# Attention with gradients on one core: o is added up two units later, one VectorE copy takes out o and dQ, and GpSimd scales dQ

## The chip, the core and the metric

The kernel runs on one core of a Trainium2 chip. A core has five engines that work side by side, each through its own queue of instructions, in the order in which they were written: TensorE (PE in the profile, its weight loads PEld), VectorE (DVE), ScalarE (ACT), GpSimd (POOL) and SyncE (SP, which here only issues DMAs). An engine waits on a semaphore when an instruction needs what another engine has not finished yet, and everything behind that instruction in the same queue waits with it. The metric is the device time of one execution in microseconds (us); less is better.

## The reference

The program computes an output and all gradients of two attention blocks that share a gradient `grad_out`: block A is linear attention, block B is softmax attention with 16 heads of 28 columns that share one K and one V (multi-query). The change touches block B alone:

```python
q = (x @ wq).reshape(B, S, H, Dh)      # S = 2048, H = 16, Dh = 28
k = x @ wk
v = x @ wv
scores = einsum("bhqd,bkd->bhqk", q, k) * Dh ** -0.5
p = softmax(scores)
o = einsum("bhqk,bkd->bhqd", p, v)
out = o.reshape(B, S, H * Dh) @ wo
```

and its backward pass: dP = dO v^T, dS = p * (dP - D) with D the row sum of dO * o, then dQ = scale * dS k, dK = dS^T q, dV = p^T dO, and the gradients of x and of the weights from them.

## The kernel before, in words

Up to about 230 us the kernel does block A and the projections of block B. Then comes the loop that the change is in (lines 905 to 1008), and after it the last weight gradients and dx (lines 1010 to 1090).

The loop works on 64 **blocks**. A block is one chunk of 256 query rows (`qc`) for one pair of heads (`pair`), numbered b = 8 qc + pair. A block takes eight **units**, one for each 256 keys (two tiles of 128). The loop variable is the unit u, and the whole order of the work is written out by hand: the loop stands in a manual schedule, each engine gets its instructions in the order of the lines, and each step has a **lag**. `due(u, lag)` gives block b when u = 8b + lag. Steps of different blocks so meet in one unit. Because the schedule repeats every eight units, it is enough to follow units 8 to 15 of a block; unit 16 is unit 8 of the next one. A step at lag 20 of one block falls in the same unit as lag 12 of the next.

What one unit u does:

- **TensorE**, first `rows_SD` (663): four matmuls for the scores S of unit u into two of three PSUM banks `SB`, and four for dP of unit w = u - 16 into the two banks `DB`. The third SB bank of the unit is called `spare`. Then on even units the first `o_dq` (914), then `onat_T` and `don_T` if they are due, then an output projection if one is due. After that, on odd units, four `dk_m` (984) for dK; on even units the second `o_dq` (986) and the `dv_mm` for dV (989).
- **ScalarE**: exp of the first score bank (927), a copy `cp` of the second half of dP (941), exp of the second score bank (973). These are the tiles `eT`, `cp`, `eT`.
- **VectorE**: dS = dP * eT for the first half of dP (939, out of the bank DB[0]), then the small steps that are due, and last a transpose of the dS tile of unit u - 18 into `dsx` (1006).
- **GpSimd**: dS for the second half, `cp` * eT (942), then the small steps that are due; in some units a copy of q (833).
- **SyncE**: every fourth unit a DMA transpose of four `eT` tiles into `eN` (975), which dV reads, and now and then others (837, 964).

The steps that take results out, for block b, with their lags before the change:

- `o_mm` (850) adds p v for unit u - 2 (first `o_dq` of an even unit) or u - 1 (second), into rows 0 to 63 of the one PSUM tile `oq`; row 0 of each head is the softmax's sum. `dq_mm` (859) adds dS k for units u - 20 and u - 19 into rows 64 to 127 of `oq`. The two take turns, so that four matmuls of 32 columns each lie beside each other.
- lag 9: VectorE copies o, 64 rows by 256, from `oq` to the SBUF tile `oTs` (955).
- lag 10: `onat_T` (788) transposes it on TensorE into the spare bank; `o_norm` (795) takes the reciprocal of the sums (800), multiplies by it and writes the normalized o into `oTs[:, 0:128]` (801, VectorE), and then on GpSimd makes `prod` = dO * o (805), `don` = dO / sum (808), and copies o over dO in `do_nat` (809).
- lag 12: `row_D` (811) sums `prod` on VectorE (813) and writes D / sum into a column of `don` on GpSimd (814). I call this last small product **Dmul**.
- lag 14: `don_T` (816) transposes `don` on TensorE into the spare bank (822), and VectorE copies the result to `doT` (829). The dP matmuls of the block begin at unit 16 and read `doT`.
- lag 20, 20, 22 and 26: the four `dv_mm` of a block (987 to 989), which read `don` and `eN`.
- lag 27: VectorE scales dQ, 64 rows by 256, out of rows 64 to 127 of `oq` into `qT_B` (958).

`oTs` has one buffer, `DB` has two banks, `SB` three.

Of the kernel before, what the change touches and what calls it, by code (L numbers as in the profile page):

```python
# [9 lines left out]
ALU = mybir.AluOpType  # L10
# [6 lines left out]
D = 448  # L17
P = 128
# [7 lines left out]
def kernel(  # L26
# [21 lines left out]
    nc = tc.nc  # L48
# [3 lines left out]
    scale = float(DH) ** -0.5  # L52
# [574 lines left out]
    NB = 64  # L627
    NU = NB * 8
    qT_B = [R1[:, g, :] for g in range(4)]
    vaug, kn, do_nat = vaug_, kn_, R2x[:, 0:NS, :]  # L630
    with ExitStack() as cs_:
# [11 lines left out]
        oq, dk_acc = (psA.tile([P, 512], F32, name="agen") for _ in range(2))  # L643

        dsT, dsx, qX, don, doT, rl, prod = ({} for _ in range(7))
# [3 lines left out]
        def eT(u):  # L649
            return ETs[u // 4 % 5][:, u % 4, :, :]  # L650

        def eN(b, c):
            return ENs[(2 * b + c // 2) % 6][:, 16 * (c % 2):16 * (c % 2) + 16, :]

        def mmt(out, lhsT, rhs, pos, start, stop):
            nc.tensor.matmul(out, lhsT=lhsT, rhs=rhs, start=start, stop=stop, tile_position=pos,  # L656
                             skip_group_check=True)

        def blk(b):
            qc, pair = divmod(b, 8)  # L660
            return qc, pair, pair // 2, pair % 2
# [29 lines left out]
        identF = pp_.tile([P, P], F32, name="identF", bufs=1)  # L691
        make_identity(nc, identF[:])
        oTs = pp_.tile([P, 256], F32, name="oTs", bufs=1)
# [3 lines left out]
        outs = {}  # L697
# [4 lines left out]
        for n in range(7):  # L702
            q_ = n + (n > 5)
            outs[400 + 8 * n] = (8 + q_ // 4, q_ % 4 * W4 - (n == 6) * W4, (q_ % 4 + 1) * W4)
        outs.update({456 + 8 * n: (10 + n // 2, n % 2 * (D // 2), (n % 2 + 1) * (D // 2)) for n in range(8)})

        def out_part(u):
            if u in (532, 536):
# [70 lines left out]
                        nc.gpsimd.dma_start(out_8[h * DH:(h + 1) * DH, :], sb[32 * j + 1:32 * j + 1 + DH, :])  # L779

        GW = [0, 0, 4, 4, 10, 10, 16, 16, 22, 22, 28, 28, 34, 34, 40, 40, 48, 48, 56, 56, 64, 64]
        onps, tps2 = {}, {}

        def due(u, lag):
            b, r = divmod(u - lag, 8)
            return b if r == 0 and 0 <= b < NB else None

        def onat_T(b, bank):
            onp = bank[:, 0:P].rearrange("p (q h c) -> p q h c", q=2, h=2)
            for qb in range(2):  # L790
                nc.tensor.transpose(onp[:, qb, :, :].rearrange("p h c -> p (h c)"), oTs[0:64, qb * P:(qb + 1) * P],
                                    identF[0:64, 0:64], tile_position=(0, 0))
            onps[b] = onp

        def o_norm(b):
            onp = onps.pop(b)
            qc, pair, g, hp = blk(b)
            r_ = pw_.tile([P, 2, 2, 1], F32, name="rl")
            os_ = oTs[:, 0:P].rearrange("p (q h c) -> p q h c", q=2, h=2)
            nc.vector.reciprocal(out=r_[:], in_=onp[:, :, :, 0:1])  # L800
            nc.vector.tensor_tensor(out=os_, in0=onp[:, :, :, :], in1=r_[:].to_broadcast([P, 2, 2, 32]), op=ALU.mult)  # L801
            rl[b] = r_
            dnv = do_nat[:, 2 * qc:2 * qc + 2, pair * 64:pair * 64 + 64].rearrange("p q (h c) -> p q h c", c=32)
            prod[b] = pw_.tile([P, 2, 2, 32], F32, name="prod", bufs=1)
            nc.gpsimd.tensor_tensor(out=prod[b][:], in0=dnv, in1=os_, op=ALU.mult)  # L805
            dn = pw_.tile([P, 2, 2, 32], BF16, name="don", bufs=3)
            don[b] = dn
            nc.gpsimd.tensor_tensor(out=dn[:], in0=dnv, in1=r_[:].to_broadcast([P, 2, 2, 32]), op=ALU.mult)
            nc.gpsimd.tensor_copy(out=dnv, in_=os_)

        def row_D(b):
            Dq = pw_.tile([P, 2, 2, 1], F32, name="Dq")
            nc.vector.tensor_reduce(out=Dq[:, :, :, 0], in_=prod[b][:], axis=AX.X, op=ALU.add)
            nc.gpsimd.tensor_tensor(out=don[b][:, :, :, 0:1], in0=Dq[:], in1=rl[b][:], op=ALU.mult)
# [16 lines left out]
        def qc_copy(eng, st, qc, g, s):  # L831
            src = qT_B[g][:, qc * 256:(qc + 1) * 256].rearrange("p (b j s) -> p b j s", b=4, s=2)[:, :, :, s]
            eng.tensor_copy(out=st.rearrange("p (b s) a j -> p b s a j", s=2)[:, :, s, :, :],  # L833
                            in_=src.unsqueeze(2).to_broadcast([P, 4, 4, 32]))
# [15 lines left out]
        def o_mm(v):  # L850
            b, tp = divmod(v, 8)
            for t2 in range(2):
                t = 2 * tp + t2
                for h in range(2):
                    mmt(oq[32 * h:32 * h + 32, 0:256], vaug[:, t, :],
                        eT(v)[:, h, t2 * 256:(t2 + 1) * 256], (0, 32 * h), t == 0, t == 15)
                yield

        def dq_mm(y):
            b, tp = divmod(y, 8)  # L860
            for t2 in range(2):
                t = 2 * tp + t2
                for h in range(2):
                    mmt(oq[64 + 32 * h:96 + 32 * h, 0:256], kn[:, t, :],
                        dsT[y][:, h, t2 * 256:(t2 + 1) * 256], (0, 64 + 32 * h), t == 0, t == 15)
                yield

        def o_dq(vs, ys):
            for v, y in zip(vs, ys):
                todo = [f(i) for f, i in ((o_mm, v), (dq_mm, y)) if 0 <= i < NU]  # L870
                for _ in range(2):
                    for g_ in todo:
                        next(g_)

        def dv_mm(dv_acc, b, h, qb):
            for c in range(4):
                rhs = eN(b, c).rearrange("p (u h t q) k -> p u h t q k", u=2, h=2,
                                                       t=2)[:, :, h, :, qb, :]
                mmt(dv_acc[32 * c:32 * c + 32, :], don[b][:, qb, h, :], rhs, (0, 32 * c),
                    b == 0 and h + qb == 0, b == NB - 1 and h + qb == 2)  # L880
# [15 lines left out]
        with tc.manual_schedule():  # L896
# [8 lines left out]
            for u in range(NU + 28):  # L905
# [5 lines left out]
                dp = DB if hasD else None  # L911
                rows_SD(u, sp, dp)
                if u % 2 == 0:
                    o_dq((u - 2,), (u - 20,))
                if (b := due(u, 10)) is not None:
                    onat_T(b, spare)
                if (b := due(u, 14)) is not None:
                    don_T(b, spare)
# [9 lines left out]
                if u == 1:  # L928
                    q_shift(pn3, shifts[3], [pd_.tile([P, 2, 512], BF16, name="dsT").rearrange("p a b -> p (a b)").bitcast(F32)
                                             for _ in range(1)])  # L930
                    dv_acc = psA.tile([P, 512], F32, name="aacc")
# [13 lines left out]
                if 0 <= gq < 4 and u < 448:  # L945
                    if gq == 0 and iq == 0:
                        qX[qq] = (pqb_ if qq % 2 else pqa_).tile([P, 4, 2, 512], BF16, name="qX")
                    if iq < 2:
                        qc_copy(nc.gpsimd, qst, qq, gq, iq)
                if (b := due(u, 12)) is not None:  # L950
                    row_D(b)
                if u == 7:
                    nc.vector.memset(oTs[64:128, :], 0.0)
                if (b := due(u, 9)) is not None:
                    nc.vector.tensor_copy(out=oTs[0:64, :], in_=oq[0:64, 0:256])  # L955
                if (b := due(u, 27)) is not None:
                    qc, pair, g, hp = blk(b)
                    nc.vector.tensor_scalar(out=qT_B[g][64 * hp:64 * hp + 64, qc * 256:(qc + 1) * 256],  # L958
                                            in0=oq[64:128, 0:256], scalar1=scale, scalar2=None, op0=ALU.mult)
                if (b := due(u, 10)) is not None:  # L960
                    o_norm(b)
                    if b in (15, 31, 47, 55, 63):
                        t0, t1 = 2 * (b // 8) - 2 * (b < 48), 2 * (b // 8) + 2
                        nc.sync.dma_start_transpose(oTq[:, 4 * (t0 % 4):4 * (t0 % 4) + 4 * (t1 - t0), :],
                                                    do_nat[:, t0:t1, :].rearrange("p q c -> p (q c)"))
# [14 lines left out]
                if u % 2:  # L980
                    b, i = divmod(u - 27, 8)
                    if 0 <= b < NB:
                        for m in range(2 * i, 2 * i + 4):
                            dk_m(b, m)
                else:
                    o_dq((u - 1,), (u - 19,))
                    b, n = divmod(u - 20, 8)
                    for k in {0: (0, 1), 2: (2,), 6: (3,)}.get(n, ()) if 0 <= b < NB else ():
                        dv_mm(dv_acc, b, k // 2, k % 2)
                y = u - 18  # L990

                if 512 <= u < 530 and u % 2 == 0:
# [9 lines left out]
                if 0 <= y < NU:  # L1002
                    b, tp = divmod(y, 8)
                    if tp == 0:
                        dsx[b] = px_.tile([P, 8, 2, 2, 256], BF16, name="dsx")
                    nc.vector.transpose(  # L1006
                        out=dsx[b][:, tp, :, :, :].rearrange("p h t c -> p (h t c)").bitcast(F32),
                        in_=dsT[y][:, :, :].rearrange("p h c -> p (h c)").bitcast(F32))
# [16 lines left out]
        for c in range(4):  # L1025
            t = dkvT[0:32, :].rearrange("p (t a i) -> p t a i", a=4, i=32)[:, :, c, :]
# [52 lines left out]
        for c in range(4):  # L1079
            r = DC_ROWS[c]  # L1080
# [41 lines left out]
```

## Time and profile before

| what | value |
|---|---|
| median of 3 runs | 1066.74 us (1066.0 to 1067.32) |
| the profiled execution: its time | 1067.99 us |
| its span, first to last instruction | 1066.3 us |
| mean granted TensorE clock | 0.998 |
| TensorE busy | 1042.2 us (98%) |
| VectorE busy | 896.1 us (84%) |
| ScalarE busy | 873.7 us (82%) |
| GpSimd busy | 781.3 us (73%) |
| first and last copy of o (line 955) start at | 230.3 and 994.5 us |

The profile's page lists busy time by engine, the span in 40 slices, the DMA queues, the chain that ended last and the costliest groups of instructions by line. A trace behind it gives each instruction's start and duration in order of time (the timeline) and what an engine waited for. Two cautions for reading it. Busy time counts the whole of each instruction, from start to finish, and consecutive instructions of one engine overlap: in the loop ScalarE starts a new instruction every 0.48 us though each is listed with some 0.6 us. So distances between starts say more than busy shares. And the 64 starts of a line that runs once in a block give the length of a block: (994.5 - 230.3) / 63 = 12.13 us.

### The profile page before, as it was taken

The page shows a single profiled execution, that of the slowest core. Times are in us where ns is not written, and L with a number is a line of the kernel's source. Part 1 is how long each engine was busy: PE and PEld are TensorE (multiplying, and loading weights), DVE is VectorE, ACT ScalarE, POOL GpSimd, SP SyncE. Part 2 cuts the span into 40 slices and gives each one's busy share as a digit, 9 for nine tenths or more (in the row PEclk, how much of TensorE's full clock was granted, in tenths as well). Part 3 has the DMA queues.
Part 4 walks back from the last instruction along what each step waited for, and adds up shares of the span by engine and source line. Part 5 has one row for each costly group of instructions (what it writes and reads, how often), then busy time and mean ns, then how long its engine had stood idle before and what let it go on. Part 6 is the DMA issues. An engine that isn't in the chain of part 4 may idle for free.

```text
span 1066.3 us, 39861 instructions
## 1 busy us (share of the span) xinstructions
PE 1042.2 (98%) x16241; PEld 476.1 (45%) x16241; DVE 896.1 (84%) x1797; ACT 873.7 (82%) x1741; POOL 781.3 (73%) x1033
## 2 busy tenths in 40 slices
PE   9999999999999999999999999999999999999998
PEld 5555555433444444444444444444444444444434
DVE  7888400459999999999999999999999999999943
ACT  6454122479999999999999999999999999999622
POOL 6001242227988898899889989988998999888881
PEclk9999999999999999999999999999999999999999
DMA  9749899079999999999999999999999999999963
GB/s 267 163 95 200 161 214 250 21 138 168 192 202 198 170 203 187 195 191 193 196 186 189 197 192 198 185 191 194 195 195 195 195 191 186 206 191 179 218 141 92
DMA packets 689936, 195.14 MB, mean 183 GB/s; under 512 B 670616, under 2 KB 687792, under 8 KB 689752
## 3 DMA queue, kind: packets, MB, share of 16 engines
q1 hardware_dynamic: 680152, 179.92, 99.2%
q0 software_dynamic: 4640, 8.71, 2.8%
q10 hardware_dynamic: 4960, 3.96, 1.3%
q8 instruction: 127, 2.08, 0.7%
q14 instruction: 57, 0.47, 0.1%
HBM read 12.60 MB, written 10.84 MB: 22 GB/s over the span
## 4 chain that ended last, share of the span: by engine, by line
PE 52%; DVE 35%; POOL 4%; issue 4%; ACT 3%; DMA 1%; DVEq 0%; POOLq 0%; ACTq 0%
PE agen L656 20%; PE agen L81 15%; DVE dsT L939 14%; DVE dsx L1006 12%; PE aacc L656 9%; PE aacc L81 7%; POOL dsT L942 4%; DVE R L958 2%; DVE oTs L801 2%; DVE oTs L955 2%; ACT cp L941 1%; DVE rl L800 1%; ACT eT L973 1%; DMA dsx<-R 1%; ACT eT L927 0%
## 5 line engine op out<-in xcount | busy, mean ns | idle before, releaser
L942 POOL TENSOR_TENSOR dsT<-cp,eT 128x512 bf16<-128x512 bf16 x512 | 588.1, 1157 | 77.3 <-ACT cp L941 68.9
L1006 DVE STREAM_TRANSPOSE dsx<-dsT 128x512 f32<-128x512 f32 x512 | 356.4, 696 | 2.4 <-POOL dsT L942 0.2
L656 PEld LDWEIGHTS <-R 32*128 32x128 bf16 (+1 forms) x9104 | 215.5, 93 | 318.3 <-issue 293.0
L939 DVE TENSOR_TENSOR dsT<-agen,eT 128x512 bf16<-128x512 f32 x512 | 338.5, 661 | 11.7 <-PE agen L656 8.4
L941 ACT ACTIVATE cp<-agen 128x512 bf16<-128x512 f32 x512 | 324.7, 634 | 12.5 <-PE agen L656 12.5
L927 ACT ACTIVATE eT<-aacc 128x512 bf16<-128x512 f32 x512 | 324.0, 633 | 11.6 <-PE aacc L656 4.7
L973 ACT ACTIVATE eT<-aacc 128x512 bf16<-128x512 f32 x512 | 330.6, 646 | 0.0
L656 PE MATMUL agen<-doT,R 32*128 32x256 bf16 x2048 | 270.9, 269 | 10.9 <-DVE dsT L939 8.2
L656 PE MATMUL aacc<-R,R 32*128 32x256 bf16 (+1 forms) x2240 | 269.7, 268 | 2.7 <-ACT eT L927 0.8
L656 PE MATMUL agen<-dsx,qX 32*32 32x512 bf16 x4096 | 267.7, 375 | 0.0
L656 PE MATMUL agen<-eT,R 128*32 128x256 bf16 x2048 | 182.0, 276 | 0.1
L656 PE MATMUL agen<-dsT,R 128*32 128x256 bf16 x2048 | 181.4, 276 | 0.1
L656 PEld LDWEIGHTS <-qX 32*32 32x32 bf16 x4096 | 79.7, 89 | 114.9 <-issue 54.3
L656 PE MATMUL aacc<-eN,don 128*32 128x512 bf16 x1024 | 97.6, 379 | 0.0
L81 PEld LDWEIGHTS <-R 128*128 128x128 bf16 (+1 forms) x517 | 41.0, 99 | 42.9 <-issue 11.1
L406 POOL COPY pk<-R 128x256 bf16<-128x256 bf16 x4 | 1.6, 397 | 75.3 <-DVE R L366 75.3
L81 PE MATMUL agen<-R,R 128*128 128x448 bf16 (+1 forms) x180 | 42.4, 363 | 0.3 <-ACT R L225 0.3
L833 POOL COPY qst<-R 128x512 bf16<-128x512 bf16 x56 | 34.2, 611 | 4.8 <-DMA qX<-qst 4.6
L805 POOL TENSOR_TENSOR prod<-R,oTs 128x128 f32<-128x128 bf16 x64 | 27.5, 430 | 9.8 <-DVE oTs L801 9.8
L656 PEld LDWEIGHTS <-don 128*32 128x32 bf16 x1024 | 34.2, 97 | 0.8
L422 DVE TENSOR_TENSOR osb<-aacc,pr 64x448 bf16<-64x448 f32 x2 | 1.2, 617 | 37.9 <-DMA out_dram<-osb 24.0
L958 DVE TENSOR_SCALAR R<-agen 64x256 bf16<-64x256 f32 x64 | 27.3, 426 | 3.6 <-PE agen L656 1.6
(231 smaller groups left out, 971.1 us busy)
## 6 DMA issues: line engine op xcount, KB each, us to landing
out_dram<-osb ACTq DMA_DIRECT2D x22, 112.0 KB
eN<-eT SPq DMA_TRANSPOSE x128
xa<-in_A_x_dram SPq DMA_DIRECT2D x8, 224.0 KB
ga<-in_grad_out_dram SPq DMA_DIRECT2D x4, 448.0 KB
xa<-in_grad_out_dram POOLq DMA_DIRECT2D x4, 448.0 KB, 5.7
out_dram<-wdq POOLq DMA_DIRECT2D x8, 224.0 KB, 3.8
eT<-in_grad_out_dram SPq DMA_DIRECT2D x4, 448.0 KB
eT<-in_B_x_dram SPq DMA_DIRECT2D x4, 448.0 KB
```

What stands on the lines that cost most here:

```text
L81: nc.tensor.matmul(out_ap, lhsT=lhsT, rhs=rhs, start=start, stop=stop, tile_position=(0, 0))
L656: nc.tensor.matmul(out, lhsT=lhsT, rhs=rhs, start=start, stop=stop, tile_position=pos, skip_group_check=True)
L801: nc.vector.tensor_tensor(out=os_, in0=onp[:, :, :, :], in1=r_[:].to_broadcast([P, 2, 2, 32]), op=ALU.mult)
L805: nc.gpsimd.tensor_tensor(out=prod[b][:], in0=dnv, in1=os_, op=ALU.mult)
L833: eng.tensor_copy(out=st.rearrange("p (b s) a j -> p b s a j", s=2)[:, :, s, :, :], in_=src.unsqueeze(2).to_broadcast([P, 4, 4, 32]))
L927: nc.scalar.activation(out=eT(u)[:, 0, :], in_=sp[0][:, :], func=ACT.Exp, scale=scale)
L939: nc.vector.tensor_tensor(out=dst[:, 0, :], in0=dp[0][:, :], in1=ew[:, 0, :], op=ALU.mult)
L941: nc.scalar.activation(out=cp[:, :], in_=dp[1][:, :], func=ACT.Copy)
L942: nc.gpsimd.tensor_tensor(out=dst[:, 1, :], in0=cp[:, :], in1=ew[:, 1, :], op=ALU.mult)
L958: nc.vector.tensor_scalar(out=qT_B[g][64 * hp:64 * hp + 64, qc * 256:(qc + 1) * 256], in0=oq[64:128, 0:256], scalar1=scale, scalar2=None, ...
L973: nc.scalar.activation(out=eT(u)[:, 1, :], in_=sp[1][:, :], func=ACT.Exp, scale=scale)
L1006: nc.vector.transpose(out=dsx[b][:, tp, :, :, :].rearrange("p h t c -> p (h t c)").bitcast(F32), in_=dsT[y][:, :, :].rearrange("p h c -> p ...
```

## The change

The diff does five things.

1. `o_mm` is done two units later: `o_dq` is called with u - 4 and u - 3 in place of u - 2 and u - 1. With that o of block b and dQ of block b - 2 are finished in the same unit. The half of `oq` that each uses alternates: o of an even block goes to rows 64 to 127 and of an odd one to rows 0 to 63, dQ to the other half.
2. At lag 11 one VectorE copy of 128 rows by 256 takes both from `oq` to `oTs`. It stands in place of the copy at lag 9 and of the scaling at lag 27. GpSimd then scales dQ of block b - 2 from `oTs` (SBUF, float32) into `qT_B`; for the last two blocks VectorE still does it out of PSUM.
3. `onat_T` and `o_norm` move from lag 10 to 12, `row_D` from 12 to 13. `don_T` and the copy to `doT` stay at lag 14.
4. The copy of o over dO in `do_nat` leaves `o_norm` and is a step of its own at lag 14 (`o_keep`); the DMA transposes of `do_nat` (five in all) move with it. Eight of the output projections start 8 units later.
5. The first `dv_mm` of a block moves from lag 20 to 18.

```diff
-        outs.update({456 + 8 * n: (10 + n // 2, n % 2 * (D // 2), (n % 2 + 1) * (D // 2)) for n in range(8)})
+        outs.update({464 + 8 * n: (10 + n // 2, n % 2 * (D // 2), (n % 2 + 1) * (D // 2)) for n in range(8)})
...
         def onat_T(b, bank):
             onp = bank[:, 0:P].rearrange("p (q h c) -> p q h c", q=2, h=2)
+            r = 64 * (1 - b % 2)
             for qb in range(2):
-                nc.tensor.transpose(onp[:, qb, :, :].rearrange("p h c -> p (h c)"), oTs[0:64, qb * P:(qb + 1) * P],
-                                    identF[0:64, 0:64], tile_position=(0, 0))
+                nc.tensor.transpose(onp[:, qb, :, :].rearrange("p h c -> p (h c)"), oTs[r:r + 64, qb * P:(qb + 1) * P],
+                                    identF[r:r + 64, r:r + 64], tile_position=(r, 0))
...
             nc.gpsimd.tensor_tensor(out=dn[:], in0=dnv, in1=r_[:].to_broadcast([P, 2, 2, 32]), op=ALU.mult)
-            nc.gpsimd.tensor_copy(out=dnv, in_=os_)
+            o_nat[b] = dnv, os_
+
+        def o_keep(b):
+            nc.gpsimd.tensor_copy(out=o_nat[b][0], in_=o_nat.pop(b)[1])
...
                 for h in range(2):
-                    mmt(oq[32 * h:32 * h + 32, 0:256], vaug[:, t, :],
-                        eT(v)[:, h, t2 * 256:(t2 + 1) * 256], (0, 32 * h), t == 0, t == 15)
+                    r = 64 * (1 - b % 2) + 32 * h
+                    mmt(oq[r:r + 32, 0:256], vaug[:, t, :],
+                        eT(v)[:, h, t2 * 256:(t2 + 1) * 256], (0, r), t == 0, t == 15)
...
                 if u % 2 == 0:
-                    o_dq((u - 2,), (u - 20,))
-                if (b := due(u, 10)) is not None:
+                    o_dq((u - 4,), (u - 20,))
+                if (b := due(u, 12)) is not None:
                     onat_T(b, spare)
                 if (b := due(u, 14)) is not None:
                     don_T(b, spare)
...
-                if (b := due(u, 12)) is not None:
+                if (b := due(u, 13)) is not None:
                     row_D(b)
                 if u == 7:
-                    nc.vector.memset(oTs[64:128, :], 0.0)
-                if (b := due(u, 9)) is not None:
-                    nc.vector.tensor_copy(out=oTs[0:64, :], in_=oq[0:64, 0:256])
-                if (b := due(u, 27)) is not None:
-                    qc, pair, g, hp = blk(b)
-                    nc.vector.tensor_scalar(out=qT_B[g][64 * hp:64 * hp + 64, qc * 256:(qc + 1) * 256],
-                                            in0=oq[64:128, 0:256], scalar1=scale, scalar2=None, op0=ALU.mult)
-                if (b := due(u, 10)) is not None:
+                    nc.vector.memset(oTs[:, :], 0.0)
+                if u % 8 == 3 and 0 <= (b := (u - 11) // 8) < NB + 2:
+                    r = 64 * (1 - b % 2)
+                    rr = slice(r, r + 64) if b < 2 else slice(0, P)
+                    if b < NB:
+                        nc.vector.tensor_copy(out=oTs[rr, :], in_=oq[rr, 0:256])
+                    if b >= 2:
+                        qc, pair, g, hp = blk(b - 2)
+                        rq = slice(64 * hp, 64 * hp + 64)
+                        if b < NB:
+                            nc.gpsimd.tensor_scalar(out=qT_B[g][rq, qc * 256:(qc + 1) * 256], in0=oTs[rq, :],
+                                                    scalar1=scale, scalar2=None, op0=ALU.mult)
+                        else:
+                            nc.vector.tensor_scalar(out=qT_B[g][rq, qc * 256:(qc + 1) * 256], in0=oq[rq, 0:256],
+                                                    scalar1=scale, scalar2=None, op0=ALU.mult)
+                if (b := due(u, 12)) is not None:
                     o_norm(b)
+                if (b := due(u, 14)) is not None:
+                    o_keep(b)
...
-                    o_dq((u - 1,), (u - 19,))
-                    b, n = divmod(u - 20, 8)
-                    for k in {0: (0, 1), 2: (2,), 6: (3,)}.get(n, ()) if 0 <= b < NB else ():
-                        dv_mm(dv_acc, b, k // 2, k % 2)
+                    o_dq((u - 3,), (u - 19,))
+                    for k, lag in enumerate((18, 20, 22, 26)):
+                        if (b := due(u, lag)) is not None:
+                            dv_mm(dv_acc, b, k // 2, k % 2)
```

`dq_mm` gets the matching rows r = 64 * (b % 2) + 32 * h.

More of the change, by code (lines that the diff above doesn't have):

```diff
@@ L781 @@
         GW = [0, 0, 4, 4, 10, 10, 16, 16, 22, 22, 28, 28, 34, 34, 40, 40, 48, 48, 56, 56, 64, 64]
-        onps, tps2 = {}, {}
+        onps, tps2, o_nat = {}, {}, {}
         def due(u, lag):
@@ L863, in dq_mm @@
                 for h in range(2):
-                    mmt(oq[64 + 32 * h:96 + 32 * h, 0:256], kn[:, t, :],
-                        dsT[y][:, h, t2 * 256:(t2 + 1) * 256], (0, 64 + 32 * h), t == 0, t == 15)
+                    r = 64 * (b % 2) + 32 * h
+                    mmt(oq[r:r + 32, 0:256], kn[:, t, :],
+                        dsT[y][:, h, t2 * 256:(t2 + 1) * 256], (0, r), t == 0, t == 15)
                 yield
```

## The prediction

> **What bounds the kernel now.** I read the page first, then the timeline of one block by engine, then the waits. The page says only that nothing is idle:
>
> ```profile
> PE 1042.2 (98%) x16241; PEld 476.1 (45%) x16241; DVE 896.1 (84%) x1797; ACT 873.7 (82%) x1741; POOL 781.3 (73%) x1033
> ...
> L942 POOL TENSOR_TENSOR dsT<-cp,eT 128x512 bf16<-128x512 bf16 x512 | 588.1, 1157 | 77.3 <-ACT cp L941 68.9
> ```
>
> From 300 to 950 us ScalarE and VectorE are busy 97 to 99% too. What a block costs is therefore read from distances. ScalarE starts something every 0.48 us when nothing holds it, three in a unit, 1.44 us a unit and 8 x 1.44 = 11.52 us a block. A block takes 12.13 us (64 copies of o between 230.3 and 994.5 us), and 12.04 us in the one I follow. So ScalarE is the floor, and all that any change can win here is about 0.5 us a block. The first exps of units 11 to 15 show where that half microsecond lies:
>
> ```profile
> 585.11 0.60 ACT L927 ACTIVATE eT<-aacc 128x512 bf16<-128x512 f32 x1
> ...
> 586.60 0.60 ACT L927 ACTIVATE eT<-aacc 128x512 bf16<-128x512 f32 x1
> ...
> 588.31 0.60 ACT L927 ACTIVATE eT<-aacc 128x512 bf16<-128x512 f32 x1
> ...
> 589.76 0.62 ACT L927 ACTIVATE eT<-aacc 128x512 bf16<-128x512 f32 x1
> ...
> 591.19 0.65 ACT L927 ACTIVATE eT<-aacc 128x512 bf16<-128x512 f32 x1
> ```
>
> 1.49, 1.71, 1.45, 1.43. The exp of unit 10 started at 583.47, so 10 to 11 took 1.64. Units 10 and 12 are long, by 0.20 and 0.27, unit 11 by 0.05, the rest is at the floor. Unit 10 is TensorE: the transposes of o (791) wait for the spare bank, which ScalarE has just read. Unit 12 is VectorE: its extra steps at lags 9 to 12 make line 939 late, and the dP matmuls wait for its bank (0.18 us at 587.99).
>
> **The part that decides: `don_T`.** Next I read GpSimd's queue in the same block:
>
> ```profile
> 584.73 1.15 POOL L942 TENSOR_TENSOR dsT<-cp,eT 128x512 bf16<-128x512 bf16 x1 [0.28 <-ACT cp L941]
> 585.85 0.43 POOL L805 TENSOR_TENSOR prod<-R,oTs 128x128 f32<-128x128 bf16 x1
> 586.23 0.40 POOL L808 TENSOR_TENSOR don<-R,rl 128x128 bf16<-128x128 bf16 x1
> 586.69 0.29 POOL L809 CAST R<-oTs 128x128 bf16<-128x128 f32 x1
> 586.94 2.27 POOL L942 TENSOR_TENSOR dsT<-cp,eT 128x512 bf16<-128x512 bf16 x2
> 589.17 0.22 POOL L814 TENSOR_TENSOR don<-Dq,rl 128x4 bf16<-128x4 f32 x1
> ```
>
> These are the large product of unit 10, then `prod`, `don` and the copy, the large products of units 11 and 12, and Dmul, which ends at 589.39. TensorE transposes `don` at 589.98, in unit 14. Dmul has 0.6 us to spare. One block in which it had none shows what happens then (columns: start, duration, instruction, idle before it and what ended that):
>
> ```profile
> 505.63 0.22 POOL L814 TENSOR_TENSOR don<-Dq,rl 128x4 bf16<-128x4 f32 x1
> ...
> 505.90 0.10 PEld L822 LDWEIGHTS <-don 128*32 128x32 bf16 x2 [0.68 <-POOL don L814]
> ...
> 506.56 0.28 PE L656 MATMUL aacc<-R,R 32*128 32x256 bf16 x1
> ...
> 506.98 0.60 ACT L927 ACTIVATE eT<-aacc 128x512 bf16<-128x512 f32 x1 [0.27 <-PE agen L656]
> ```
>
> TensorE stands at `don_T`; behind it in its queue are the second `o_dq`, `dv_mm` and the scores of unit 15. ScalarE runs dry and starts unit 15 1.13 us after Dmul's end (505.85 to 506.98), 1.87 us after unit 14 (505.11).
>
> The change takes two units from this path. o is ready at lag 10 in place of 8 and everything up to `prod` moves with it; `row_D` moves by one unit, `don_T` not at all. In GpSimd's queue Dmul of lag 13 stands behind the large product of unit 13, which starts only when ScalarE has made `cp` of unit 13. I lay out the new block, with time 0 at the first exp of unit 11:
>
> - Large product of unit 11: from 1.18 (590.94 - 589.76, the same step in unit 14). The next start is 1.12 later (584.73 to 585.85): 2.30.
> - **New: scaling of dQ.** No such step is in the trace. It has 256 elements per partition, one input. Above: the large product, 1.157 us, twice the elements and two inputs. Below: the copy of 128 elements (809), 0.289 us. The nearest row is GpSimd's copy of 128x256 (406), 0.397 us, same count and one input; I take 0.40 and end at 2.70.
> - Large product of unit 12: its `cp` is there at 1.44 + 1.18 = 2.62, so it starts at 2.70. `prod` 3.82, `don` 4.20.
> - Large product of unit 13 comes 0.46 after `don` (586.23 to 586.69): 4.66, and its `cp` was there by 1.44 + 1.64 + 1.18 = 4.26. Dmul 5.78, its end 6.00.
> - TensorE wants `don_T` 0.22 after the exp of unit 14 (589.98 - 589.76): 1.44 + 1.64 + 1.44 + 0.22 = 4.74. It waits some 1.26 us, in every block.
> - The exp of unit 15: 6.00 + 1.13 = 7.13. Four units at the floor (1.445 from 591.19 to 594.07) to unit 11 of the next block: 5.78.
>
> The block is 12.91 us, against 12.04 now: **+0.87 us**. The floor units in it already hold the whole gain of the change, the disappearance of the 0.27 and 0.05 at units 11 and 12. Blocks 1 to 62 pay: block 0 has no large product yet, block 63 has no exps left to delay. 62 x 0.87 = 54 us. On the profiled execution's own 1067.99 us (span 1066.3, 1.7 outside it) that gives 1122, on the median of 1066.74 **1121 us**.
>
> The dQ scaling moves this sum alone: at 0.29 the large product of unit 12 starts at 2.62, when `cp` lets it, block 12.83, +49 us, 1116; at 1.157 it starts at 3.46, block 13.67, +101 us, 1168. Two GpSimd rows with two inputs (430 ns for 128 elements, 1157 for 512) give 0.67 for 256 by a straight line, +71 us, 1138. That is why the range reaches up further than down.
>
> [...]
>
> **The other parts.**
>
> - VectorE loses 62 scalings of 426 ns; the copy grows from 64 to 128 rows with as many elements per row. I cost it at the old 399 ns: the product out of PSUM over 128 rows (939, 512 elements) takes 661, less than twice that. The 0.43 us saved per block is worth at most the 0.32 us of ScalarE idle that line 939 causes, and it is counted.
> - VectorE gets two waits. Line 801 writes `oTs`, which GpSimd's scaling reads until 2.70; it would come at about 2.50 (1.06 after the exp, 596.62 - 595.56). Behind it wait the unit's transpose and line 939 of unit 13. The row sum at lag 13 waits for `prod`, 4.25, instead of about 3.9. Both are covered: TensorE stands until 6.0, and VectorE has caught up by then. Without that cover they cost 0.2 + 0.35 us a block.
> - `onat_T` meets the same spare bank in unit 12 as it did in unit 10 and waits the same 0.2 us; TensorE's work in unit 15 is held anyway.
> - `o_keep` adds nothing: the same 0.29 us copy, now behind unit 14's large product, in a stretch where ScalarE is late.
> - `dv_mm` at lag 18: no wait for `eN` is in the list from 300 to 950 us. SyncE spends 5.5 us on each of its transposes, one in 6 us, and lags by under 3 us; it is done with a tile some 7 us after the tile's last exp (592.83 to 599.64), and lag 18 is 11 units, 16 us, after. Unit 10 gets eight such matmuls, unit 12 loses four: unit 12 with eight took 1.36 us on TensorE (586.17 to 587.53), below the floor.
> - The `do_nat` transposes are issued four units later, behind the same transposes of `eT` in SyncE's queue; their first reader is 10 units behind as the output projections move too, 14 for the last. No cost. GpSimd's output DMAs (0.58 us) come at unit 8, three units before the scaling, each with some 0.3 us idle.
>
> **Rivals.**
>
> - *GpSimd is the bound* (0.14). The scaling costs nearer to the large product, or copies of q (833, 0.61 us, in units 14 and 15 of half the blocks) leave it late at unit 11. Each 0.1 us goes straight into the chain, 6 us in all: 1138 to 1168. Against it: after Dmul it has 0.7 us idle before `cp` of unit 15.
> - *Faster* (0.09). Dmul reaches `don_T` in time. It decides whether Dmul ends by 4.7 instead of 6.0, which needs it ahead of the large product of unit 13 (1.12) and a short scaling. GpSimd's spans are called rough, and that is what speaks for it; the order in the trace follows the lines, which speaks against. Then the 0.32 us come back: 62 x 0.32 = 20, 1047.
> - *Neither* (0.05). `don_T` is in time, but the two VectorE waits are no longer covered: 0.2 + 0.35 - 0.32 = 0.23 at most, 14 us, and about nothing if `prod` is as early: 1067 to 1081.
>
> **Chances.** The forecast, 1121 with 1105 to 1138, has 0.72. The range takes in most of the GpSimd rival and stops a little below the forecast's own end, for a wait shorter than laid out: 1092 to 1152. Measurement can tell about 0.2% here. Faster 0.09, within 0.2% 0.03, slower 0.88.
>
> **What would show it.** The wait of line 822 for Dmul, 3.6 us over 7 times now, should be 60 to 95 us over some 60. The distance between the copies of o goes from 12.13 to about 13.0 us. GpSimd's new step should take 0.40 us, the large copy 0.40. ScalarE's idle time should lie ahead of the first exp, in unit 15. I am wrong if `don_T` waits little, or if it waits and the exps of unit 15 do not.

## The result, and the profile after

| | before | after |
|---|---|---|
| median | 1066.74 us (4 runs) | 1152.55 us (4 runs, 1149.88 to 1153.85) |
| ratio | | 1.0802, 95% interval 1.078 to 1.0823 |
| profiled execution: span | 1066.3 us | 1150.1 us |
| mean granted TensorE clock | 0.998 | 0.999 |
| first and last copy of o start at | 230.3 and 994.5 us | 230.6 and 1076.7 us |
| block: distance between copies, mean | 12.13 us | 13.43 us |

The change costs 85.8 us. The forecast was 1121, slower by 54: the direction and the place were right, the amount was too small, and the range ended at 1152. (13.43 - 12.13) x 63 = 82 us of it lie in the loop's steady part.

Line numbers have moved: in the changed kernel 933, 947 and 989 are ScalarE's exps and `cp`, 945 and 948 the two dS products, 964 the large copy, 969 GpSimd's scaling of dQ, 802 the normalized o, 806 `prod`, 809 `don`, 818 Dmul, 826 `don_T`, 833 the copy to `doT`. The page of the changed kernel, busy time and two of the groups:

```profile
PE 1042.9 (91%) x16232; PEld 460.0 (40%) x16241; DVE 884.2 (77%) x1735; ACT 884.4 (77%) x1741; POOL 834.3 (73%) x1095
...
L948 POOL TENSOR_TENSOR dsT<-cp,eT 128x512 bf16<-128x512 bf16 x512 | 591.5, 1156 | 114.0 <-ACT cp L947 96.7
...
L969 POOL TENSOR_SCALAR R<-oTs 64x256 bf16<-64x256 f32 x62 | 52.4, 845 | 2.7
```

TensorE and ScalarE do the same work as before in a longer span, so their shares fall. GpSimd's large products cost the same 1156 ns and wait longer for `cp`. The new step takes 845 ns; the forecast had 400. The list of waits over the whole span (total, times, longest):

```profile
PEld L826 <- POOL don L818: 70.8, 63, 1.3
DVE oTs L802 <- POOL R L969: 50.8, 62, 0.9
ACT eT L933 <- PE agen L656: 42.6, 73, 0.7
ACT cp L947 <- PE agen L656: 40.2, 75, 1.8
PE aacc L656 <- DVE oTs L802: 36.1, 61, 0.7
```

The first line is the wait that the forecast set its sum on, 60 to 95 us over some 60 times. The second and the fifth it did not have, or not so. GpSimd's queue in one block, from the large product of unit 11 to Dmul:

```profile
606.60 1.16 POOL L948 TENSOR_TENSOR dsT<-cp,eT 128x512 bf16<-128x512 bf16 x1 [0.20 <-ACT cp L947]
607.73 0.84 POOL L969 TENSOR_SCALAR R<-oTs 64x256 bf16<-64x256 f32 x1
608.55 1.15 POOL L948 TENSOR_TENSOR dsT<-cp,eT 128x512 bf16<-128x512 bf16 x1
609.66 0.42 POOL L806 TENSOR_TENSOR prod<-R,oTs 128x128 f32<-128x128 bf16 x1
610.05 0.39 POOL L809 TENSOR_TENSOR don<-R,rl 128x128 bf16<-128x128 bf16 x1
610.41 1.14 POOL L948 TENSOR_TENSOR dsT<-cp,eT 128x512 bf16<-128x512 bf16 x1
611.52 0.20 POOL L818 TENSOR_TENSOR don<-Dq,rl 128x4 bf16<-128x4 f32 x1
```

The order is the one laid out in the forecast, step for step, and GpSimd is not idle from 606.60 to the end of Dmul. On ScalarE, the first exps (933) of units 11 to 15 of the same block, `cp` of unit 13 (947), and the first exp of unit 11 of the next block:

```profile
605.35 0.69 ACT L933 ACTIVATE eT<-aacc 128x512 bf16<-128x512 f32 x1
...
606.81 0.69 ACT L933 ACTIVATE eT<-aacc 128x512 bf16<-128x512 f32 x1
...
608.45 0.60 ACT L933 ACTIVATE eT<-aacc 128x512 bf16<-128x512 f32 x1
609.44 0.60 ACT L947 ACTIVATE cp<-agen 128x512 bf16<-128x512 f32 x1 [0.39 <-PE agen L656]
...
610.67 0.60 ACT L933 ACTIVATE eT<-aacc 128x512 bf16<-128x512 f32 x1
...
612.86 0.60 ACT L933 ACTIVATE eT<-aacc 128x512 bf16<-128x512 f32 x1 [0.61 <-PE agen L656]
...
618.65 0.69 ACT L933 ACTIVATE eT<-aacc 128x512 bf16<-128x512 f32 x1
```

Unit 13 (608.45) takes 2.22 us in place of 1.44, because its `cp` starts late; unit 14 (610.67) takes 2.19, because TensorE stands (waits idle) at `don_T`. Unit 12 takes the 1.64 of the unit with the transposes of o, and the others are at the floor. Unit 15 starts 1.14 after Dmul's end (611.72), and unit 11 of the next block at 618.65, 5.79 later. The forecast had 1.13 and 5.78.

### The profile page after: what moved, and what is told of

The parts are those of the page before. It is cut to its first block, busy times and chain, and to the rows that moved or that the text cites. A ratio compares the mean times of both kernels' runs of the same rounds, so it can differ in the third digit from the quotient of the medians.

```text
span 1150.1 us, 40033 instructions
## 1 busy us (share of the span) xinstructions
PE 1042.9 (91%) x16232; PEld 460.0 (40%) x16241; DVE 884.2 (77%) x1735; ACT 884.4 (77%) x1741; POOL 834.3 (73%) x1095
## 4 chain that ended last, share of the span: by engine, by line
PE 34%; POOL 29%; ACT 17%; issue 13%; DVE 7%; DMA 0%; POOLq 0%; ACTq 0%; DVEq 0%
POOL dsT L948 21%; PE agen L81 13%; ACT cp L947 10%; PE agen L656 7%; PE aacc L81 7%; ACT eT L989 5%; PE aacc L656 5%; POOL R L969 5%; DVE dsx L1022 2%; DVE dsT L945 2%; PE aacc L826 1%; POOL prod L806 1%; POOL don L809 1%; ACT eT L933 1%; DVE oTs L802 1%
## 5 line engine op out<-in xcount | busy, mean ns | idle before, releaser
L948 POOL TENSOR_TENSOR dsT<-cp,eT 128x512 bf16<-128x512 bf16 x512 | 591.5, 1156 | 114.0 <-ACT cp L947 96.7
L947 ACT ACTIVATE cp<-agen 128x512 bf16<-128x512 f32 x512 | 325.0, 635 | 43.1 <-PE agen L656 40.2
L656 PEld LDWEIGHTS <-R 128*32 128x32 bf16 (+1 forms) x9104 | 204.2, 94 | 349.2 <-issue 321.2
L656 PE MATMUL aacc<-R,R 32*128 32x256 bf16 (+1 forms) x2240 | 259.3, 267 | 39.4 <-DVE oTs L802 36.1
L656 PE MATMUL agen<-doT,R 32*128 32x256 bf16 x2048 | 284.9, 271 | 2.9 <-DVE dsT L945 2.0
L656 PE MATMUL agen<-eT,R 128*32 128x256 bf16 x2048 | 188.7, 276 | 0.2 <-PE aacc L656 0.2
L656 PE MATMUL agen<-dsT,R 128*32 128x256 bf16 x2048 | 188.5, 276 | 0.0
L826 PE MATMUL aacc<-identB,don 128*32 128x128 bf16 x256 | 18.5, 224 | 53.1 <-POOL don L818 28.7
L802 DVE TENSOR_TENSOR oTs<-aacc,rl 128x128 f32<-128x128 f32 x64 | 18.7, 292 | 50.9 <-POOL R L969 50.8
L969 POOL TENSOR_SCALAR R<-oTs 64x256 bf16<-64x256 f32 x62 | 52.4, 845 | 2.7
L833 DVE COPY doT<-aacc 64x256 bf16<-64x256 bf16 x64 | 18.5, 288 | 36.3 <-PE aacc L826 18.6
```

The costliest lines, as they stand in the source:

```text
L826: nc.tensor.transpose(tp2[q:q + 32, qb * P:(qb + 1) * P], don[b][:, qb, h, :], identB[:, :], tile_position=(0, q))
L947: nc.scalar.activation(out=cp[:, :], in_=dp[1][:, :], func=ACT.Copy)
L948: nc.gpsimd.tensor_tensor(out=dst[:, 1, :], in0=cp[:, :], in1=ew[:, 1, :], op=ALU.mult)
L969: nc.gpsimd.tensor_scalar(out=qT_B[g][rq, qc * 256:(qc + 1) * 256], in0=oTs[rq, :], scalar1=scale, scalar2=None, op0=ALU.mult)
```

## The experiments

The theory going in was the forecast's chain with the measured step in it: scaling, large product, `prod`, `don`, large product, Dmul, `don_T`, scores of unit 15, all in one line. The main rival came from the trace above: line 802 writes `oTs` and waits for GpSimd's scaling, which still reads it (50.8 us in the list above); the scores of unit 13 wait until 802 has read the spare PSUM bank (36.1 us), and `cp` of unit 13 is late (40.2 us). The other rival was that the lags alone cost it. Ratios are to the kernel before the change on the same chip.

**1. The size of the step.** The scale goes into `kn` once before the loop, and GpSimd copies where it scaled:

```diff
-    nc.gpsimd.tensor_scalar(out=qT_B[g][rq, ...], in0=oTs[rq, :], scalar1=scale, scalar2=None, op0=ALU.mult)
+    nc.gpsimd.tensor_copy(out=qT_B[g][rq, ...], in_=oTs[rq, :])
```

> The changed kernel, but kn, the keys' tile that dQ is made with, is multiplied by the scale once before the loop, so that GpSimd only copies dQ (64x256, float32 to bfloat16) at the same place where it scales it now. Theory (a chain on GpSimd sets the block: dQ step of unit 11, large product of unit 12, prod, don, large product of unit 13, Dmul, then don_T and the scores of unit 15): the step falls from the measured 0.845 us to about the 0.40 that the forecast took, every 0.1 us of it is worth 6 us, so 1152.5 - 62 x 0.445 = 1125 us (1119 to 1132). Rival (the lags alone cost it, whatever GpSimd's step takes): unchanged, 1145 to 1153.

Measured: 1121.36 us, 1.0502 (1.0481 to 1.0522). The group of the step in that run:

```profile
L972 POOL CAST R<-oTs 64x256 bf16<-64x256 f32 x62 | 24.3, 392 | 2.0
```

With the step at 392 ns the kernel takes what the forecast said for 400; that the two agree to less than 1 us is in part luck, as the run's own executions lie between 1120.4 and 1123.4. The rival falls: the lags were left alone. The saving is 31 us for 62 x 0.453 = 28 us of GpSimd time, so the step lies on the chain with its whole length.

**2. Dmul ahead of the large product.** `row_D` is called in unit 13 ahead of GpSimd's product:

```diff
                     nc.vector.tensor_tensor(out=dst[:, 0, :], in0=dp[0][:, :], in1=ew[:, 0, :], op=ALU.mult)
+                    if (b := due(u, 13)) is not None:
+                        row_D(b)
...
                     nc.gpsimd.tensor_tensor(out=dst[:, 1, :], in0=cp[:, :], in1=ew[:, 1, :], op=ALU.mult)
```

> The changed kernel, but in unit 13 the row sum and Dmul are written ahead of GpSimd's large product instead of behind it; nothing else moves. Theory (GpSimd's chain through don_T): Dmul ends about 1.1 us earlier, don_T hardly waits, unit 15 then starts at the ScalarE floor after unit 14, which is itself still late by about 0.8 us through the wait of unit 13: a block is 0.75 us shorter, 62 x 0.75 = 46, 1106 us (1095 to 1116). Rival (the wait of line 802 for the dQ scaling, which holds the spare PSUM bank and with it the scores and cp of unit 13, is what costs the time): that wait is untouched, and the time stays within 15 us of 1152.

Measured: 1109.56 us, 1.0388 (1.037 to 1.0407). The waits from 300 to 1000 us:

```profile
DVE oTs L802 <- POOL R L971: 45.7, 54, 1.0
...
PE aacc L656 <- DVE oTs L802: 33.2, 54, 0.8
ACT cp L949 <- PE agen L656: 26.4, 55, 0.8
...
PEld L826 <- POOL don L818: 6.1, 27, 0.2
```

The stand at `don_T` is nearly gone (6.1 us), the waits of the rival are as large as ever, and 43 us come back. Unit 13 still takes 2.29 us on the mean, and unit 14 is back at 1.45. What the rival's waits cost was hidden behind the stand until then.

**3. The rival's wait taken away.** The normalized o gets its own tile (and the halves of `doT` share one buffer, to make room):

```diff
+        oNs = pp_.tile([P, P], F32, name="oNs", bufs=1)
...
-            os_ = oTs[:, 0:P].rearrange("p (q h c) -> p q h c", q=2, h=2)
+            os_ = oNs[:, :].rearrange("p (q h c) -> p q h c", q=2, h=2)
```

> The changed kernel, but the normalized o gets an SBUF tile of its own (room for it comes from keeping the two halves of doT in one buffer), so that line 802 no longer waits for GpSimd's dQ scaling and the spare bank is free in time for unit 13. Theory (GpSimd's chain): the order and the sum on GpSimd are the same, the wait moves from unit 13 to don_T of unit 14, and the time stays: 1140 to 1153 us. Rival (the spare bank's wait): the 0.4 to 0.8 us of unit 13 go, 62 x 0.6 = 37, 1115 us or less.

Measured: 1167.21 us, 1.093 (1.091 to 1.095), 15 us more than the changed kernel. The waits from 300 to 1000 us do what the theory says: that of the tile's writer is gone, and the one at `don_T` has grown from 58.6 to

```profile
PEld L828 <- POOL don L820: 95.8, 51, 2.0
```

The theory's 1140 to 1153 us and the rival's 1115 or less both miss the time: that it rises neither had. The reason is TensorE's clock. The mean granted clock of this run is 0.981, in every repetition 0.981 or 0.982, where the other kernels have 0.997 to 1.0. One block of it in slices of 1 us (columns: slice, length, busy time of PE, PEld, DVE, ACT and POOL with counts, granted TensorE clock, DMA share, GB/s):

```profile
331.00:332.00 1.00, 0.07 (x4) 0.00 (x0) 0.87 (x3) 1.00 (x3) 1.00 (x3) 1.00 1.17 217
332.00:333.00 1.00, 0.20 (x10) 0.21 (x14) 0.61 (x2) 0.30 (x1) 1.00 (x3) 1.00 1.16 218
333.00:334.00 1.00, 1.00 (x24) 0.27 (x14) 0.81 (x2) 0.00 (x0) 1.00 (x2) 0.61 1.07 204
334.00:335.00 1.00, 1.00 (x16) 0.28 (x12) 0.80 (x3) 0.74 (x2) 0.06 (x1) 0.50 0.07 19
335.00:336.00 1.00, 1.00 (x14) 0.15 (x7) 0.60 (x1) 0.83 (x2) 0.58 (x1) 0.50 0.00 0
336.00:337.00 1.00, 1.00 (x36) 0.58 (x36) 0.32 (x1) 0.37 (x1) 0.57 (x1) 0.68 0.00 0
```

TensorE has nothing to do for 1.7 us in one piece, and then its clock is at 0.5 for 3.4 us. Units 14 and 15 of that block take 3.54 and 2.37 us, against 3.16 and 1.45 two blocks later, where the clock holds (the blocks are of a longer and a shorter kind in turn, so like is compared with like): 1.3 us. Twelve such dips lie in the loop, and from the fifth block on the blocks together take 15.3 us more than in the changed kernel, as much as the whole rise. In the changed kernel the same time is lost in two stands of 0.5 to 0.9 us, and the clock stays at 1.00.

The blocks without a dip settle the question. Most take 13.54 and 13.30 us in turn, in this run and in the changed kernel alike. In the longer kind units 13 and 14 took 2.35 and 2.30 us, now 1.49 and 3.16, and the sum of 4.65 is the same. So the rival is out: its wait is real, and when it is taken away the time moves to `don_T` and nothing is won.

**4. The scaling out of the chain.** Own tile, and the scaling in unit 9 (lag 33):

```diff
-                        if b < NB:
-                            nc.gpsimd.tensor_scalar(out=qT_B[g][rq, ...], in0=oTs[rq, :], ...)
...
+                if (b := due(u, 33)) is not None and b < NB - 2:
+                    nc.gpsimd.tensor_scalar(out=qT_B[g][rq, ...], in0=oTs[rq, :], ...)
```

> The changed kernel with an own tile for the normalized o, and GpSimd's dQ scaling moved out of the chain, from lag 27 to lag 33 (unit 9, behind that unit's large product). Dmul stays behind the large product of unit 13. Theory (GpSimd's chain): by the forecast's own sum with nothing for the scaling, a block of 12.83 us against 13.43 measured, 62 x 0.6 = 37, 1115 us (1105 to 1125); don_T still waits about 1.2 us in each block. Rival (the scaling or the bank wait is all there is to it): 1045 to 1070 us.

Measured: 1117.06 us, 1.0465 (1.0441 to 1.0489). The rival's 1045 to 1070 falls. The chain without the step gives what the forecast's lower end said (1116), with the same 845 ns spent elsewhere on the same engine.

**5. Both out: late scaling and Dmul first.**

> The kernel with the own tile and the dQ scaling at lag 33 (which took 1117 us), and besides Dmul written ahead of the large product in unit 13. Theory (two things lie on the chain, the scaling ahead of it and the large product ahead of Dmul; without both, ScalarE is the floor again): a block of 11.52 + 0.2 (transposes of o) + 0.1 to 0.3, that is 11.8 to 12.0 against 12.13 before the change: 1046 to 1060 us, faster than before the change. Rival (o two units later, with four consecutive units full of small steps, costs of itself): 1067 us or more.

Measured: 1083.0 us, 1.0143 (1.013 to 1.0156). Here the theory falls and the rival's 1067 or more holds: with scaling and large product off the chain ScalarE is not at its floor. The waits from 300 to 1000 us:

```profile
PEld L828 <- POOL don L820: 24.5, 57, 0.7
DVE Dq L819 <- POOL prod L808: 21.6, 57, 0.6
```

VectorE stops in each block for `prod` and TensorE for Dmul, 0.4 us each. In some blocks GpSimd also comes late to unit 11, and VectorE's copy waits for the scaling (4.0 us over 6 times).

**6. VectorE's scaling put back.** VectorE scales dQ out of PSUM in unit 11 and copies 64 rows of o; GpSimd has no such step, and Dmul is again behind:

```diff
-                    rr = slice(r, r + 64) if b < 2 else slice(0, P)
+                    rr = slice(r, r + 64)
...
-                        if b < NB:
-                            nc.gpsimd.tensor_scalar(...)
-                        else:
+                        if True:
                             nc.vector.tensor_scalar(out=qT_B[g][rq, ...], in0=oq[rq, 0:256], ...)
```

> The changed kernel, but VectorE scales dQ out of PSUM in unit 11, beside a copy of o alone (64 rows), as it did before the change; GpSimd has no dQ step. Lags and Dmul as in the changed kernel. Theory (GpSimd's chain, its floor without a dQ step): VectorE's 0.43 us a block is hidden behind the stand at don_T, 1117 us as with the scaling at lag 33 (1110 to 1125). Rival (VectorE's time counts in this order too): 62 x 0.43 = 27 us more, 1144.

Measured: 1115.3 us, 1.0448 (1.0433 to 1.0463), as the theory had it: against run 4, VectorE's extra 0.43 us a block costs nothing in this order.

**7. The same with Dmul first.** Only the lags and the order of the small steps now differ from the kernel before.

> The same as the run with VectorE's scaling in unit 11, and Dmul ahead of the large product in unit 13. Only the lags and the order of the small steps then differ from the kernel before the change. Theory (the stand at don_T gone, VectorE with as much work as before the change): about the time before, 1060 to 1075 us; against the run with the own tile, the late scaling and Dmul first it shows what taking the scaling from VectorE is worth, 10 to 20 us. Rival (VectorE's scaling costs nothing, as it stood in the shadow of other waits): the same time as that run.

Measured: 1085.07 us, 1.0159 (1.0146 to 1.0173), against 1083.0 in run 5. The rival of this run holds: giving VectorE's scaling to GpSimd is worth about 2 us here, not 10 to 20. And the later o, with VectorE's scaling and Dmul ahead of the product, costs 1.6% though no engine has more work: units 12 and 13 take 1.81 and 1.79 us on the mean, against 1.65 and 1.45 before, while units 10 and 11 fall from 1.62 and 1.53 to 1.47 and 1.46.

**8. A short late step.** Run 5 with the scaled `kn` of run 1, so that GpSimd copies at lag 33.

> The run with own tile, late dQ step and Dmul first, with kn scaled once ahead of the loop, so that GpSimd's late step is a copy of about 0.39 us instead of a scaling of 0.845. Theory (GpSimd is no bound there, a step at lag 33 has slack): within 5 us of the same kernel with the scaling. Rival (GpSimd's total is the bound, some 11 us of work in a block of 12): 62 x 0.45 = 28 us less.

Measured: 1076.74 us, 1.0077 (1.0064 to 1.0091): 6.3 us less, just over the theory's 5 and far from the rival's 28. VectorE's copy in unit 11 now waits once, 0.2 us in all. GpSimd's total is not the bound, but it is no longer without effect.

**9. `don_T` a unit later.** Run 8 with

```diff
-                if (b := due(u, 14)) is not None:
+                if (b := due(u, 15)) is not None:
                     don_T(b, spare)
```

and the copy to `doT` likewise.

> The run with own tile, late copy of dQ, scaled kn and Dmul first (1077 us), with don_T and the copy to doT moved from lag 14 to 15 as well, don_T behind the scores of the unit. Theory now (what is left is the lack of slack at the end: o two units later leaves prod, row sum, Dmul, don_T and doT in three units in a row, and the doT copy holds the spare bank that the next unit's scores need; a step more of room gives that back): about 0.3 us a block at units 13 to 16, 62 x 0.3 = 19 us, 1050 to 1066 us. Rival (the dP matmuls of unit 16 then wait for doT, the wait only moves): 1072 us or more.

Measured: 1073.87 us, 1.0062 (1.0049 to 1.0074). 3 us of the expected 11 or more, and the rival's 1072 or more holds: the wait has moved. The dP matmuls now wait, though for their bank and not for `doT`, that is for VectorE's dS product of line 950 (from 300 to 1000 us):

```profile
PE agen L659 <- DVE dsT L950: 15.7, 57, 0.6
```

VectorE waits for `prod` as before (18.2 us over 56 times).

**10. One lag alone, in the kernel before.**

```diff
-                if (b := due(u, 12)) is not None:
+                if (b := due(u, 13)) is not None:
                     row_D(b)
```

> The kernel before the change, with one edit: row_D at lag 13 in place of 12. Nothing is added or taken away; o, the scaling and all else stay. Theory (Dmul behind the large product of unit 13 makes TensorE stand at don_T): by the rows of the kernel before, Dmul then ends 589.47 + 1.16 + 0.22 = 590.85, unit 15 starts 1.13 later at 591.98 instead of 591.19, 0.79 us a block, 62 x 0.79 = 49, 1116 us (1105 to 1122). Rival (the order on GpSimd matters only together with the later o): within 10 us of 1067.

Measured: 1107.93 us, 1.038 (1.0363 to 1.0397). The sum was 8 us too high. Most of that is Dmul, which ends 5.57 and 5.70 us after the first exp of unit 11 in turn, where the sum had 5.74 (590.85 - 585.11). But this edit of one digit, without any new work, costs 41 us, and the rival falls. Two lines of its trace, GpSimd in units 11 to 14 (the first row holds the products of units 11 to 13):

```profile
615.99 3.56 POOL L942 TENSOR_TENSOR dsT<-cp,eT 128x512 bf16<-128x512 bf16 x3
619.50 0.22 POOL L814 TENSOR_TENSOR don<-Dq,rl 128x4 bf16<-128x4 f32 x1
```

Dmul stands behind three products where the kernel before had two.

**11 and 12. Looking for an order that gains.** Run 9 with the row sum and Dmul at the head of unit 14, once with the short copy of dQ and once with the scaling itself.

> The run with own tile, late copy of dQ, scaled kn and don_T at lag 15 (1074 us), but the row sum and Dmul stand at the head of unit 14 (on VectorE behind the transpose of unit 13, on GpSimd behind the large product of unit 13) instead of inside unit 13. Theory (what is left is VectorE's 0.3 us wait for prod inside unit 13, which makes line 939 late and through the dP bank the units 14 to 16; with don_T at 15 Dmul has room to come later): 0.2 to 0.4 us a block, 1050 to 1062 us, faster than the kernel before the change. Rival (don_T at 15 then waits for Dmul, the wait moves on): 1072 us or more.

> The same kernel, but GpSimd scales dQ at lag 33 (0.845 us) and kn is left as it was: all that the change does, in an order that gives each step room. Theory: some 6 us more than the run with the copy, as between the two runs with Dmul first (1083 and 1077), through GpSimd being late at unit 11 in the blocks with copies of q: 1056 to 1068 us, about the kernel before. Rival (a step of 0.845 us on GpSimd has slack anywhere off the chain): the same as the run with the copy, within 2 us.

Measured: 1072.1 us, 1.0047 (1.0033 to 1.0061), and 1075.3 us, 1.0072 (1.0057 to 1.0086). VectorE no longer waits for `prod` (no such line in the list), but unit 15 is then long, 1.80 us on the mean: `don_T` waits for Dmul, and the dK matmuls and the next scores start behind it. In the run with the copy, from 300 to 1000 us:

```profile
PEld L831 <- POOL don L823: 12.4, 57, 0.4
```

So the first run's rival (1072 or more) holds, and both times miss the theory's ranges. The two differ by 3 us, between the 2 and the 6 of the second run's rival and theory. None of these runs beats the kernel before.

## Why the prediction was wrong

**What failed is one term of the sum: "The nearest row is GpSimd's copy of 128x256 (406), 0.397 us, same count and one input; I take 0.40."** The step takes 0.845. The chain of the forecast, each start counted from the first exp of unit 11, against the block at 605.35:

| step | forecast | measured |
|---|---|---|
| scaling starts | 2.30 | 2.38 |
| large product of unit 12 | 2.70 | 3.20 |
| `prod` | 3.82 | 4.31 |
| large product of unit 13 | 4.66 | 5.06 |
| Dmul ends | 6.00 | 6.37 |
| first exp of unit 15 | 7.13 | 7.51 |
| block | 12.91 | 13.30 |

Each row behind the scaling is late by 0.37 to 0.50 us, and the order is the forecast's. With 0.845 in the sum the block would have been 12.91 + 0.445 = 13.36 and the time 1121 + 62 x 0.445 = 1149. Run 1 shows the other direction: with the step at 392 ns the time is 1121.36. The last 3 to 4 us lie in a thing that the forecast did not have. The block of the table is of the shorter kind; in the one before it, which takes 13.55, the scaling starts 2.50 and the large product of unit 12 3.43 after the first exp of unit 11. The mean of 13.30 and 13.54 is 0.06 above 13.36, 62 x 0.06 = 4 us. Why every second block is longer is not known.

The bounds for the step were right, 0.29 and 1.157. The value was taken from the row that looked most alike, a plain copy. The profiled rows show that the operation can count more than the size: on the same 64x256, float32 to bfloat16, GpSimd's copy takes 392 ns and its scaling by a constant 845. The copy is level with VectorE's copy of as many elements out of PSUM, 392 ns against 399; the scaling is not, 845 against VectorE's 426. The range then cut off the upper end of the bounds (1168) at 1152, and the result lies half a microsecond outside.

Point by point, the rest:

- *ScalarE is the floor, and there is little to win.* Right: outside units 13 and 14 every unit takes 1.43 to 1.48 or the 1.64 of the unit with the transposes of o. The half microsecond of gain could not be had even without the stand: giving VectorE's scaling to GpSimd was worth 2 us (run 7 against 5), and with GpSimd's shorter copy in its place 8 (run 7 against 8), not 62 x 0.32 = 20.
- *TensorE stands at `don_T` in every block.* Right: 63 times, 1.1 us each. The decisive argument, that `row_D` goes a unit later past a large product while `don_T` stays, is shown alone by run 10, and undone by run 2.
- *The two new VectorE waits are covered.* Right in effect, but too small and without where it leads. The wait of 802 is 0.8 us a block, not 0.2 (0.36 with the short step of run 1, so most of the excess is the same mis-sized term), and it is not quiet: 802 holds the spare PSUM bank, the scores of unit 13 need it, and ScalarE stops at `cp`. That is early enough to be made good before `don_T` (in run 3 it is gone, and a block at full clock is as long as ever), but where the stand is gone it shows (run 2 against run 5, 27 us, in which the scaling on GpSimd goes as well).
- *The large copy costs what the small one did.* Right: 415 ns against 399.
- *`o_keep`, the earlier `dv_mm`, the later transposes of `do_nat` cost nothing.* From 300 to 1000 us the list of waits after names none of them. They were not tried apart, so this is not shown.
- *The rival "GpSimd is the bound", 1138 to 1168, had 0.14.* It named the mechanism that the result fell to, a scaling nearer to the large product, and its price, 6 us for each 0.1 us.
- *The rival "faster".* Run 2 grants its condition, Dmul ahead of the product, and run 4 a scaling out of the way; both together (run 5) leave 1083, or 1077 with a short step (run 8). So even there it would not have been faster: the forecast's 1047 for that case left out that o two units later puts `prod`, row sum, Dmul, `don_T` and `doT` into three units in a row.

The loss of 85.8 us divides along the runs like this: 18 for the later o with Dmul first (1085.1 - 1067, run 7), 30 for Dmul behind the product (run 6 - run 7), 37 for GpSimd's scaling in the chain (after - run 6). The shares depend on the order in which they are taken: with the scaling in the chain Dmul's place is worth 43 (after - run 2) and the scaling then 24 (run 2 - run 7), as each hides a part of the other. Each is a difference of two medians and good to 2 us or so.

What stays open in part is why runs 8, 9, 11 and 12 end just above the kernel before, where most blocks take 12.02 to 12.04 us. In run 8 every second block takes 12.07, and the others mostly 12.27, with unit 15 at 1.79 us instead of 1.60. In runs 9, 11 and 12 most blocks take 12.16; in run 11 units 10 and 11 are at the floor, but unit 12 takes 1.64 with the transposes of o, and unit 15 gives back at `don_T` what they won. Lags between the old and the new ones for o (one unit later instead of two) were not tried.

## What to carry to other kernels

When a step is moved later and its reader is not, walk the queue of every engine between the two and count the long instructions that it now stands behind: here one 1.16 us product, passed by one lag, was worth 41 us in 1067, though no engine got more work. Work taken from one busy engine and given to another with 27% idle is not free if the other's queue is the chain (here 37 us, the changed kernel against run 6): look where in that queue it lands. And price an operation that the trace does not show by its own kind, not by its size (here 392 ns for the copy and 845 for the scaling of as many elements); if no row of its kind exists, the range has to reach to the slower bound.

## What the runs showed of the hardware

- GpSimd, 64x256 float32 to bfloat16: copy 392 ns on the mean (run 1), scaling by a constant 845 ns (838 to 864, the changed kernel), 62 of each.
- TensorE's granted clock in run 3 (0.981 on the mean) is at 0.5 twelve times in the loop, about 3.4 us each time: in the slices above from 333.2 to 336.6 us, and nine windows of 13 us that hold one whole dip have a mean of 0.87. In the block of the slices TensorE ran no matmul for 1.72 us ahead of `don_T` at 332.80, and the dip starts 0.4 us after it. From 300 to 1000 us that run has 51 waits at `don_T`, 95.8 us in all and 2.0 at the longest, and ten of the dips; what sets the waits near a dip apart from the others was not shown. In the changed kernel no wait at `don_T` is longer than 1.3 us, and the granted clock is 1.00 from 240 to 1000 us, as it is in the kernel before.
- A PSUM bank handed on from unit to unit made waits that no line of the code names: in the changed kernel GpSimd's read of an SBUF tile held VectorE for 0.8 us a block, the bank that VectorE had not read held TensorE's scores for 0.6, and these held ScalarE's `cp` for 0.5 (from 300 to 1000 us: 43.7 us over 53 times, 31.5 over 53, 24.3 over 53).
